# Second mixture's up products: four arms of columns instead of seven widths, and no turned path for few tokens

## The chip, the cores and the metric

The kernel runs on one core of a Trainium2 chip. The metric is the device time of one execution in microseconds; the time before is the median of three runs. The profile shows one further execution with its own time. The engines are TensorE (PE; its weight loads stand apart as PEld), VectorE (DVE), ScalarE (ACT), GpSimd (POOL) and the queue of SyncE (SP), which starts the transfers.

## The reference

Attention without softmax, a dense feed-forward layer, and a mixture of eight experts follow on each other. The change lies in the mixture:

```python
logits = x @ w_gate                       # 2304 tokens, 512 features, 8 experts
expert_idx = np.argmax(logits, axis=1)
gate_w = probs[np.arange(N), expert_idx]  # probs: softmax of the logits
for i in range(N):                        # at most capacity = 576 tokens per expert
    e = expert_idx[i]
    if counts[e] < capacity:
        disp[e, counts[e]] = x[i]; pos[i] = counts[e]; counts[e] += 1; keep[i] = True
h = np.maximum(np.einsum('ecd,edf->ecf', disp, w1), 0.0)   # up: 512 -> 1024
y = np.einsum('ecf,efd->ecd', h, w2)                       # down: 1024 -> 512
out[i] = gate_w[i] * y[expert_idx[i], pos[i]]              # for kept tokens
```

How many tokens an expert gets is known only on the chip. With these inputs the router sends 52, 625, 167, 219, 614, 160, 391 and 76 tokens to experts 0 to 7, of which at most 576 are kept. The kernel starts with an expert chosen while the tokens are still routed and goes round from there; here that is expert 1, so the order is 576, 167, 219, 576, 160, 391, 76 and 52 tokens.

## The kernel before

The first part (attention, feed-forward, routing) is not touched. In the second part each expert goes through the same code, written out once for each of the eight places e = 0 to 7. Its 1024 hidden features are eight blocks f of 128.

Products are made in a float32 type that TensorE multiplies in one pass, with each operand split into a high and a low half; a product is three passes (high by high, high by low, low by high) over four chunks of the 512 features, so 12 products of a 128x128 weight block with the tokens' columns. `part` (line 810) writes these 12 for one block f and a number of columns.

`up(e, f)` makes one block of the up product in one of three double banks of PSUM, `hb`, taken in turn. Since the number of tokens n[e] is known only at run time, `widths` writes seven arms, for 256, 304, 352, 400, 448, 512 and 576 columns (the last is two parts, 256 and 320), under a tree of three levels of comparisons; a register `off` tells the evacuation where in the bank the columns begin. `up2(e, i)` holds two blocks f and is itself one arm of a branch: with at most 128 tokens, the other arm multiplies the other way round (`turned`: the tokens are the stationary operand, 256 columns of weights the moving one), copies the result to SBUF with ScalarE and turns it back with two transposes on TensorE.

`put_g` evacuates a block: ScalarE writes the high half of relu(h) (line 874), then VectorE the low half (line 875), for all 576 columns, or 128 in the turned arm. `put_last` (line 880) has ScalarE copy the 64 columns of each half of the expert's last token tile, which are packed side by side for `down`. It waits for VectorE's half. `next_pair` splits two weight tiles of a later product: ScalarE casts them to the high half (line 190), GpSimd subtracts (line 194). `up2` is called four times for each expert, with a `next_pair` after the first three.

After the up blocks come `tr_x` (transposes of the next expert's tokens, line 789), three `next_pair`, and `down` for each token tile of 128 (24 products of 512 columns, line 907, or 16 if the tile holds at most 64 tokens), then two `next_pair`. `nothing` (line 778) is a small product for arms that have nothing to do. Place e = 0 is special: its first 256 columns were made early, and `up_rest` (columns from 256 on) runs in the arm that is taken here; the other arm holds eight calls of `up`.

All queues run in the order in which the code is written (`manual_schedule`).

Of the kernel before, what the change touches and what calls it, by code (L numbers as in the profile page):

```python
# [7 lines left out]
F32 = mybir.dt.float32  # L8
F32R = mybir.dt.float32r
BF16 = mybir.dt.bfloat16  # L10
I32 = mybir.dt.int32
I64 = mybir.dt.int64
AF = mybir.ActivationFunctionType
ALU = mybir.AluOpType
# [5 lines left out]
P = 128  # L20


PASSES = ((0, 0), (0, 1), (1, 0))
# [3 lines left out]
def attn_moe_kernel(ctx: ExitStack, tc: tile.TileContext, cap, kp, vp, qt, gn, wm, wg, wgt, w1, w2, ident, tri, out):  # L27
    nc = tc.nc
    B, NPAIR, _, NCH, _ = kp.shape
# [3 lines left out]
    KD = DM // P  # L33
    NF = wm.shape[0]
    E, NF2 = w1.shape[0], w1.shape[1] * 2
# [6 lines left out]
    NARROW, BANK, HALF = 256, 512, P // 2  # L42
# [4 lines left out]
    const = ctx.enter_context(tc.tile_pool(name="const", bufs=1))  # L47
# [7 lines left out]
    id_sb = const.tile([P, P], F32, name="id_sb")  # L55
    tri_sb = const.tile([P, 2, P], BF16, name="tri_sb")
    cnt = const.tile([P, E], F32, name="cnt")
    cnt_i = const.tile([P, E], I32, name="cnt_i")
    off_i = const.tile([P, E], I32, name="off_i")
    last_i = const.tile([P, E], I32, name="last_i")  # L60

    ek_i = const.tile([P, E], I32, name="ek_i")
# [460 lines left out]

    LAG, LEAD = 2, 4
    HOT = 9
    LEVELS = (NARROW, 304, 352, 400, 448, BANK, cap)
    units = []

    with tc.manual_schedule(engines={mybir.EngineType.SP}):
# [146 lines left out]
        for s in range(len(units)):  # L676
            j, f = units[s]
# [37 lines left out]
        v = nc.vector  # L715
# [3 lines left out]
        v.tensor_scalar(cnt, cnt, 1.0, -1.0, op0=ALU.max, op1=ALU.add)  # L719
        v.tensor_copy(last_i, cnt)  # L720
        v.tensor_scalar(last_i, last_i, 7, 7, op0=ALU.logical_shift_right, op1=ALU.logical_shift_left)
        v.tensor_scalar(off_i, cnt, float(BANK - 1), float(BANK - NARROW), op0=ALU.is_gt, op1=ALU.mult)
    ph1.close()


    g2_p = ctx.enter_context(tc.tile_pool(name="g2_p", bufs=1))
    x2_p = ctx.enter_context(tc.tile_pool(name="x2_p", bufs=1))
    xr_p = ctx.enter_context(tc.tile_pool(name="xr_p", bufs=4))
    ht_p = ctx.enter_context(tc.tile_pool(name="ht_p", bufs=1))
    me_p = ctx.enter_context(tc.tile_pool(name="me_p", bufs=2))  # L730
    wpool3.append(ctx.enter_context(tc.tile_pool(name="wpool3", bufs=2)))

# [1 line left out]
    hb = [psum[0].tile([P, 2 * BANK], F32, name=f"hb{i}") for i in range(3)]  # L734
    bk = [psum[1].tile([P, 512], F32, name=f"bk{i}") for i in range(2)]
# [3 lines left out]
    x2 = x2_p.tile([P, 2, KD, cap], F32R, name="x2")  # L739
# [18 lines left out]
    with tc.manual_schedule():  # L758
# [9 lines left out]
        ET = mybir.EngineType  # L768
# [7 lines left out]
        def nothing(ps, w):  # L776

            nc.tensor.matmul(ps[:w, :E], lhsT=tri_sb[:, 0, :w], rhs=tri_sb[:, 1, :E], start=True, stop=True)
# [20 lines left out]
        def w1_at(e, i, a, c):  # L799

            return we1[e, 2 * i + c // 2][:, a, c % 2 * 2 * P:(c % 2 + 1) * 2 * P]

        def part(e, f, h, o, w, x=x2):


            order = [(c, a, m) for c in range(KD) for a, m in PASSES]
            if f == 0:
                order = [(c, a, m) for a, m in ((0, 0), (1, 0), (0, 1)) for c in range(KD)]
            for k, (c, a, m) in enumerate(order):
                nc.tensor.matmul(  # L810
                    h, lhsT=w1_at(e, f // 2, a, c)[:, f % 2 * P:(f % 2 + 1) * P], rhs=x[:, m, c, o:o + w],
                    start=k == 0, stop=k == 3 * KD - 1,
                )

        def widths(e, levels, arm):

            mid = len(levels) // 2
            if not mid:
                return arm(levels[0])
            with tc.If(n[e] > levels[mid - 1]) as c:  # L820
                widths(e, levels[mid:], arm)
            with c.Else():
                widths(e, levels[:mid], arm)

        def up(e, f):

            h = hb[(e * NF2 + f) % 3]

            def arm(w):
                if w > BANK:  # L830
                    part(e, f, h[:, BANK - NARROW:BANK], 0, NARROW)
                    part(e, f, h[:, BANK:BANK + w - NARROW], NARROW, w - NARROW)
                else:
                    part(e, f, h[:, :w], 0, w)

            widths(e, LEVELS, arm)
            put_g(f, h[:, bass.ds(off[e], cap)], slice(0, cap))

        turned_sb = [ht_p.tile([P, 2 * P], F32, name=f"turned{i}") for i in range(2)]

        def turned(e, i):

            s = (bk[i % 2] if i else hb[e * NF2 % 3][:, BANK:])[:, :2 * P]
            order = [(c, a, m) for c in range(KD) for a, m in PASSES]
            for k, (c, a, m) in enumerate(order):
                nc.tensor.matmul(
                    s, lhsT=x2[:, a, c, :P], rhs=w1_at(e, i, m, c), start=k == 0, stop=k == len(order) - 1,
                )
            return s

        def up2(e, i):

            with tc.If(nall[e] > P) as many:  # L853
                up(e, 2 * i)
                up(e, 2 * i + 1)
            with many.Else():
                if i == 0:
                    nc.scalar.copy(turned_sb[0], turned(e, 0))
                if i + 1 < NF2 // 2:
                    s = turned(e, i + 1)  # L860
                hs = [hb[(e * NF2 + 2 * i + k) % 3][:, :P] for k in range(2)]
                for k, h in enumerate(hs):
                    nc.tensor.transpose(h, turned_sb[i % 2][:, k * P:(k + 1) * P], id_sb)
                if i + 1 < NF2 // 2:
                    nc.scalar.copy(turned_sb[(i + 1) % 2], s)
                for k, h in enumerate(hs):
                    put_g(2 * i + k, h, slice(0, P))
            for f in range(2 * i, 2 * i + 2):
                put_last(f, bass.ds(last[e], HALF))

        def put_g(f, src, cols):

            g = g2[f][:, :, cols]
            nc.scalar.activation(out=g[:, 0], in_=src, func=AF.Relu)  # L874
            nc.vector.scalar_tensor_tensor(  # L875
                out=g[:, 1], in0=src, scalar=0.0, in1=f32(g[:, 0]), op0=ALU.max, op1=ALU.subtract
            )

        def put_last(f, cols):
            nc.scalar.copy(gl[f], f32(g2[f][:, :, cols]))  # L880
# [71 lines left out]
        for f in range(3):  # L952
# [5 lines left out]
            skip_runtime_bounds_check_because="an expert has no more than all tokens",  # L958
        )
        _, n = nc.values_load_multi_w_load_instructions(  # L960
            cnt_i[0:1, :], engines=[PE], min_val=0, max_val=cap,
            skip_runtime_bounds_check_because="the counts are clamped to the capacity on the chip",
        )
        _, nall = nc.values_load_multi_w_load_instructions(
            cnt_i[0:1, :], engines=[PE, ET.Activation, ET.DVE, ET.Pool], min_val=0, max_val=cap,
            skip_runtime_bounds_check_because="the counts are clamped to the capacity on the chip",
        )

        _, off = nc.values_load_multi_w_load_instructions(
            off_i[0:1, :], engines=[ET.Activation, ET.DVE], min_val=0, max_val=BANK - NARROW,  # L970
            skip_runtime_bounds_check_because="the offsets are one of two numbers",
        )

        _, last = nc.values_load_multi_w_load_instructions(
            last_i[0:1, :], engines=[ET.Activation], min_val=0, max_val=(cap - 1) // P * P,
            skip_runtime_bounds_check_because="the counts are clamped to the capacity on the chip",
# [11 lines left out]
        for e in range(E):  # L988
            if e + 1 < E:
                for t in range(4):  # L990
                    load_x(e + 1, t)
            if e == 0:
                with tc.If(early > NARROW - 1) as done:
                    for f in range(NF2):
                        up_rest(f)
                with done.Else():
                    tr_x(0, 0)
                    tr_x(0, 1)
                    for f in range(NF2):
                        up(0, f)  # L1000
                        put_last(f, bass.ds(last[0], HALF))
            else:
                for i in range(NF2 // 2):
                    up2(e, i)
                    if i < NF2 // 2 - 1:
                        next_pair((AP, AP))
            if e + 1 < E:
                tr_x(e + 1, 0)
                tr_x(e + 1, 1)
                for t in range(4, NST):  # L1010
                    load_x(e + 1, t)
            if e:
                next_pair((AP, AP))
            next_pair((AP, AP))
            next_pair((AP, AP))
            down(e, 0)
            if e + 1 < E:
                rest_x(e + 1, range(2, NST))
            with tc.If(nall[e] > P) as some:  # L1019
                down(e, 1)  # L1020
            with some.Else():
                nothing(hb[((e + 1) * NF2 + 2) % 3], P)
            next_pair((AP, AP))
            next_pair((AP, AP))
            down_rest(e, 2)
# [50 lines left out]
```

## Time and profile before

| | before |
|---|---|
| median of 3 runs | 810.14 us (810.14 to 811.97) |
| profiled execution | 804.85 us |
| its span, first to last instruction | 803.1 us |
| mean granted TensorE clock | 0.968 of full |
| TensorE busy | 729.3 us, 91% |
| weight loads busy | 648.0 us, 81% |
| VectorE, ScalarE, GpSimd busy | 371.1, 310.5, 291.5 us |
| DMA | 102.82 MB, 128 GB/s on average |

A stage is read by its start and end in the span, the engine's busy time in it, and what ended the idle time between. "issue" means that the profile shows nothing that the engine waited for. A name in an arrow, as in [1.80 <-DVE g L875], is what the profile infers as the last thing waited for, after so many microseconds of idleness. Some matmul records can be missing, so a count of 98 may stand for a few more.

### The profile page before, as it was taken

Reading aid. Unit: us, or ns where it says so; the run is one execution under the profiler, and the core shown is the slowest. Engines: PE = TensorE matmul, PEld = TensorE weight load, DVE = VectorE, ACT = ScalarE, POOL = GpSimd, SP = SyncE. Lnnn points to the kernel's source line nnn. Section 1 sums busy time; section 2 is a strip of 40 time slices with the busy share of each in tenths; the row PEclk is TensorE's granted clock in tenths of the full one; section 3 lists DMA queues with packets and bytes.
Section 4 is the critical chain, followed back from the end, with each engine's and each line's share of the span. In section 5 each row is a group of like instructions: output and inputs, shape, how many; then the busy total and the mean of one; then the engine's idle time right before and its main releaser. Section 6 shows DMA issues by size and latency. Waiting matters only on the chain. (4 is left out here: it accounts for less than half of the span.)

```text
span 803.1 us, 12019 instructions
## 1 busy us (share of the span) xinstructions
PE 729.3 (91%) x3988; PEld 648.0 (81%) x3988; DVE 371.1 (46%) x829; ACT 310.5 (39%) x650; POOL 291.5 (36%) x288
## 2 busy tenths in 40 slices
PE   6788999999999999999999899997879997879663
PEld 6777999989999998899989788876768976777553
DVE  2999767279924943494469434202212202221101
ACT  2555454242223322322334533424635444544422
POOL 2575233030212002102104923253847373667440
PEclk9899999999999999999999999999969999999779
DMA  9937898020212012001004723353444454455400
GB/s 332 373 123 275 290 302 292 27 76 1 105 69 77 1 66 83 27 1 53 13 1 158 233 97 106 100 165 109 143 164 148 165 154 136 129 182 164 152 20 11
DMA packets 38044, 102.82 MB, mean 128 GB/s; under 512 B 4451, under 2 KB 4707, under 8 KB 37920
## 3 DMA queue, kind: packets, MB, share of 16 engines
q1 hardware_dynamic: 34912, 91.99, 35.0%
q0 software_dynamic: 3008, 9.10, 3.0%
q8 instruction: 87, 1.43, 0.8%
q14 instruction: 37, 0.30, 0.1%
HBM read 77.78 MB, written 23.91 MB: 127 GB/s over the span
## 5 line engine op out<-in xcount | busy, mean ns | idle before, releaser
L273 PE MATMUL pk<-xT,w 128*128 128x384 f32 x1152 | 223.1, 341 | 7.5 <-POOL w L183 4.6
L292 PE MATMUL pk<-w,g 128*128 128x512 f32 x864 | 218.3, 394 | 2.5 <-ACT g L284 2.5
L273 PEld LDWEIGHTS pk<-xT,w 128*128 128x128 f32 x1152 | 201.6, 188 | 17.3 <-POOL w L183 5.9
L194 POOL TENSOR_TENSOR w<-st,w 128x512 fp32r<-128x512 f32 x128 | 161.2, 1294 | 120.2 <-ACT w L190 120.2
L292 PEld LDWEIGHTS pk<-w,g 128*128 128x128 f32 x864 | 160.2, 188 | 31.7 <-ACT g L284 3.1
L810 PE MATMUL hb<-x,w 128*128 128x256 f32 (+2 forms) x672 | 105.5, 316 | 24.5 <-issue 11.3
L810 PEld LDWEIGHTS hb<-x,w 128*128 128x128 f32 x672 | 99.4, 203 | 29.9 <-issue 14.4
L875 DVE SCALAR_TENSOR_TENSOR g<-hb,g 128x576 fp32r<-128x576 f32 (+3 forms) x72 | 41.4, 586 | 147.6 <-ACT g L874 147.6
L281 ACT ACTIVATE rr<-pk 128x384 f32<-128x384 f32 x96 | 47.1, 491 | 154.2 <-PE pk L273 154.0
L283 DVE TENSOR_TENSOR pk<-pk,rr 128x384 f32<-128x384 f32 x96 | 54.0, 563 | 75.0 <-ACT rr L281 74.2
L102 POOL DMA_INDIRECT disp<-y,sli x18 | 19.0, 1058 | 173.5 <-DVE sli L409 52.9
L354 DVE SCALAR_TENSOR_TENSOR junk<-y,wgb 128x512 f32<-128x512 f32 x120 | 77.9, 684 | 0.6 <-ACT y L312 0.6
L190 ACT CAST w<-st 128x512 fp32r<-128x512 f32 x128 | 71.5, 620 | 11.6 <-DMA st<-in_w 11.2
L284 ACT CAST g<-pk 128x384 fp32r<-128x384 f32 x96 | 46.0, 479 | 72.2 <-DVE pk L283 71.8
L285 DVE TENSOR_TENSOR g<-pk,g 128x384 fp32r<-128x384 f32 x96 | 53.3, 556 | 36.3 <-ACT g L284 36.1
L183 POOL TENSOR_TENSOR w<-cf,w 128x512 fp32r<-128x512 f32 x32 | 46.8, 1481 | 61.4 <-ACT w L182 56.8
L907 PE MATMUL hb<-w,g 128*128 128x512 f32 x264 | 65.8, 407 | 3.2 <-DVEq L946 2.9
L907 PEld LDWEIGHTS hb<-w,g 128*128 128x128 f32 x264 | 50.2, 194 | 15.3 <-DVEq L946 3.2
L874 ACT ACTIVATE g<-hb 128x576 fp32r (+3 forms) x72 | 36.1, 515 | 66.3 <-PE hb L810 63.4
L102 POOL DMA_INDIRECT out<-o,meta x22 | 21.3, 968 | 56.5 <-DVEq L1019 22.6
L923 DVE SCALAR_TENSOR_TENSOR o<-bk,meta,o 64x512 f32<-64x512 f32 x3 | 2.3, 751 | 70.5 <-ACT o L922 50.6
L239 POOL TENSOR_SCALAR ms<-ss 128x8 f32<-128x8 f32 x18 | 4.6, 253 | 76.2 <-DVE ss L237 75.9
(134 smaller groups left out, 651.6 us busy)
## 6 DMA issues: line engine op xcount, KB each, us to landing
st<-in_w SPq DMA_DIRECT2D x64, 512.0 KB, 3.9
st<-in_wm SPq DMA_DIRECT2D x32, 512.0 KB, 6.9
disp<-zrow SPq DMA_DIRECT2D x9, 1028.0 KB, 11.2
xr<-disp SPq DMA_DIRECT2D x32, 257.0 KB, 4.8
k<-in_kp SPq DMA_DIRECT2D x16, 320.0 KB, 4.4
v<-in_vp SPq DMA_DIRECT2D x16, 320.0 KB, 4.1
q<-in_qt SPq DMA_DIRECT2D x18, 256.0 KB, 3.2
out<-zrow SPq DMA_DIRECT2D x9, 512.0 KB, 8.3
```

Source lines behind the costliest of these rows:

```text
L183: nc.gpsimd.tensor_tensor(w[:, 1, :], o, f32(w[:, 0, :]), op=ALU.subtract)
L190: nc.scalar.copy(w[:, 0, :], s[:, i, :])
L194: e.tensor_tensor(w[:, 1, :], s[:, i, :], f32(w[:, 0, :]), op=ALU.subtract)
L273: nc.tensor.matmul(h, lhsT=wi[f][:, a, c * P:(c + 1) * P], rhs=xT[j][:, m, c, :], start=n == 0, stop=n == 3 * KD - 1,)
L281: nc.scalar.activation(out=r, in_=h, func=AF.Relu)
L283: nc.vector.tensor_tensor(h, h, r, op=ALU.mult)
L284: nc.scalar.copy(g[:, 0, :], h)
L285: nc.vector.tensor_tensor(g[:, 1, :], h, f32(g[:, 0, :]), op=ALU.subtract)
L292: nc.tensor.matmul(ysets[j == 1][i], lhsT=g[:, a, i * P:(i + 1) * P], rhs=wo[f][:, m, :], start=f == 0 and n == 0, stop=f == NF - 1 and n ...
L354: nc.vector.scalar_tensor_tensor(out=junk, in0=yt[j * TB + i][:, :DM], scalar=1.0, in1=wgb[e // 2][:, e % 2, :], op0=ALU.mult, op1=ALU.mul ...
L810: nc.tensor.matmul(h, lhsT=w1_at(e, f // 2, a, c)[:, f % 2 * P:(f % 2 + 1) * P], rhs=x[:, m, c, o:o + w], start=k == 0, stop=k == 3 * KD - 1,)
L907: nc.tensor.matmul(ps[:k, :], lhsT=lhs(f, a), rhs=we2[e, f][:, b, :], start=n == 0, stop=n == len(passes) * NF2 - 1,)
```

## The change

The seven widths become four arms in a tree on TensorE alone: at most 128 tokens, 128 columns; else 256 columns and then, if there are more tokens, 160 further columns (up to 416) or 320 (up to 576). The turned arm, its two SBUF tiles, its transposes and copies go, as does the branch around a pair of blocks that all four compute engines took. The offset register goes, since the columns always begin at the same place. The evacuation always covers 576 columns. `put_last` of a block now stands right behind its evacuation.

```diff
-    LEVELS = (NARROW, 304, 352, 400, 448, BANK, cap)
+    MIDDLE = 416
...
-        def widths(e, levels, arm):
-
-            mid = len(levels) // 2
-            if not mid:
-                return arm(levels[0])
-            with tc.If(n[e] > levels[mid - 1]) as c:
-                widths(e, levels[mid:], arm)
-            with c.Else():
-                widths(e, levels[:mid], arm)
-
         def up(e, f):
 
-            h = hb[(e * NF2 + f) % 3]
-
-            def arm(w):
-                if w > BANK:
-                    part(e, f, h[:, BANK - NARROW:BANK], 0, NARROW)
-                    part(e, f, h[:, BANK:BANK + w - NARROW], NARROW, w - NARROW)
-                else:
-                    part(e, f, h[:, :w], 0, w)
-
-            widths(e, LEVELS, arm)
-            put_g(f, h[:, bass.ds(off[e], cap)], slice(0, cap))
...
-        def up2(e, i):
-
-            with tc.If(nall[e] > P) as many:
-                up(e, 2 * i)
-                up(e, 2 * i + 1)
-            with many.Else():
...
-            for f in range(2 * i, 2 * i + 2):
-                put_last(f, bass.ds(last[e], HALF))
+            h = hb[(e * NF2 + f) % 3][:, BANK - NARROW:]
+            with tc.If(n[e] <= P) as few:
+                part(e, f, h[:, :P], 0, P)
+            with few.Else():
+                part(e, f, h[:, :NARROW], 0, NARROW)
+                with tc.If(n[e] <= NARROW) as less:
+                    nothing(h[:, NARROW:], P)
+                with less.Else():
+                    with tc.If(n[e] <= MIDDLE) as some:
+                        part(e, f, h[:, NARROW:MIDDLE], NARROW, MIDDLE - NARROW)
+                    with some.Else():
+                        part(e, f, h[:, NARROW:cap], NARROW, cap - NARROW)
+            put_g(f, h[:, :cap], slice(0, cap))
...
                 for i in range(NF2 // 2):
-                    up2(e, i)
+                    for f in range(2 * i, 2 * i + 2):
+                        up(e, f)
+                        put_last(f, bass.ds(last[e], HALF))
                     if i < NF2 // 2 - 1:
                         next_pair((AP, AP))
```

On TensorE, one block f of an expert in the order of the program before (`hb` is the PSUM bank, `x` the tokens, `w` the weights; x12 counts the products; each stands for a weight load and a matmul):

```order
L820 COMPARE_AND_BRANCH x3
L810 MATMUL hb_4469<-x_4489,w 128x256 x12
L810 MATMUL hb_4469<-x_4489,w 128x320 x12
L820 UNCONDITIONAL_BRANCH
L810 MATMUL hb_4469<-x_4489,w 128x512 x12
L820 UNCONDITIONAL_BRANCH
...
L810 MATMUL hb_4469<-x_4489,w 128x352 x12
L820 UNCONDITIONAL_BRANCH
L810 MATMUL hb_4469<-x_4489,w 128x304 x12
L820 UNCONDITIONAL_BRANCH
L810 MATMUL hb_4469<-x_4489,w 128x256 x12
```

The same block after the change, line numbers being those of the changed kernel:

```order
L815 COMPARE_AND_BRANCH
L807 MATMUL hb_4463<-x_4484,w 128x128 x12
L815 UNCONDITIONAL_BRANCH
L807 MATMUL hb_4463<-x_4484,w 128x256 x12
L819 COMPARE_AND_BRANCH
L775 LDWEIGHTS tri_sb
L775 MATMUL hb_4463<-tri_sb 128x8
L819 UNCONDITIONAL_BRANCH
L822 COMPARE_AND_BRANCH
L807 MATMUL hb_4463<-x_4484,w 128x160 x12
L822 UNCONDITIONAL_BRANCH
L807 MATMUL hb_4463<-x_4484,w 128x320 x12
```

Eight arms of 12 products in the program became four and a dummy product; with 256 columns the arm stood last before and now stands second.

On ScalarE, the second pair of blocks of an expert before (`g` is the evacuated block, `gl` the copy for the last tile, L865 the copy of the turned arm):

```order
L874 ACTIVATE g_2_4475<-hb_4469 128x576
L874 REGISTER_ALU
L874 ACTIVATE g_3_4476<-hb_4470 128x576
L853 UNCONDITIONAL_BRANCH
L865 COPY turned_4508<-bk_4471 128x256
L874 ACTIVATE g_2_4475<-hb_4469 128x128
L874 ACTIVATE g_3_4476<-hb_4470 128x128
L853 UNCONDITIONAL_BRANCH
L880 ISA
L880 COPY gl_4483<-g_2_4475 128x128
L880 ISA
L880 COPY gl_4484<-g_3_4476 128x128
```

And after:

```order
L831 ACTIVATE g_2_4470<-hb_4464 128x576
L815 UNCONDITIONAL_BRANCH
L837 ISA
L837 COPY gl_4478<-g_2_4470 128x128
L831 ACTIVATE g_3_4471<-hb_4465 128x576
L815 UNCONDITIONAL_BRANCH
L837 ISA
L837 COPY gl_4479<-g_3_4471 128x128
```

The copies moved from behind both evacuations of a pair to behind each of them, and the arm of 128 columns is gone from ScalarE's program.

## Rows read from the trace of the kernel before

**Rows 1.** The page: TensorE's busy time, the large instruction queue, GpSimd's weight differences.

```profile
PE 729.3 (91%) x3988; PEld 648.0 (81%) x3988; DVE 371.1 (46%) x829; ACT 310.5 (39%) x650; POOL 291.5 (36%) x288
...
q8 instruction: 87, 1.43, 0.8%
...
L194 POOL TENSOR_TENSOR w<-st,w 128x512 fp32r<-128x512 f32 x128 | 161.2, 1294 | 120.2 <-ACT w L190 120.2
```

**Rows 2.** Up stages of e1, e2, e4, e5, e6: busy PE, PEld, DVE, ACT, POOL; clock; DMA.

```profile
544.80:564.40 19.60, 14.30 (x98) 13.00 (x97) 6.05 (x8) 9.61 (x20) 8.45 (x8) 0.91 0.23 67
574.70:601.40 26.70, 18.86 (x99) 17.50 (x99) 5.97 (x8) 11.88 (x24) 15.41 (x15) 0.68 0.53 172
...
667.90:688.60 20.70, 12.82 (x97) 11.77 (x96) 6.06 (x8) 9.73 (x20) 8.69 (x9) 1.00 0.26 73
699.90:723.00 23.10, 18.83 (x99) 17.14 (x98) 6.21 (x9) 12.63 (x26) 15.09 (x17) 1.00 0.60 180
744.60:764.50 19.90, 10.46 (x64) 9.16 (x63) 4.00 (x11) 11.35 (x33) 9.78 (x10) 0.76 0.43 143
```

**Rows 3.** Timeline of PE, e1's up stage and down products: start, length, instruction, idle before.

```profile
544.78 3.99 PE L810 MATMUL hb<-x,w 128*128 128x256 f32 x32
...
553.16 1.69 PE L810 MATMUL hb<-x,w 128*128 128x256 f32 x12 [1.64 <-DVE g L875]
...
562.83 1.70 PE L810 MATMUL hb<-x,w 128*128 128x256 f32 x12 [1.11 <-issue]
...
565.16 5.79 PE L907 MATMUL hb<-w,g 128*128 128x512 f32 x24
...
570.83 3.97 PE L907 MATMUL hb<-w,gl 128*128 128x512 f32 x16
```

**Rows 4.** Timeline of PE, e0's remaining columns and e3's up stage.

```profile
501.23 14.33 PE L810 MATMUL hb<-x,w 128*128 128x320 f32 x96
516.98 1.08 PE L789 MATMUL bk<-id_sb,xr 128*128 128x128 f32 x8 [1.42 <-issue]
...
614.98 25.82 PE L810 MATMUL hb<-x,w 128*128 128x256 f32 x192
```

**Rows 5.** DMA queues, windows 544.8:565.2 and 615:641.4: packets, MB, share.

```profile
q8 instruction: 6, 0.10, 2.2%
...
q8 instruction: 7, 0.11, 1.7%
```

**Rows 6.** Timeline of ScalarE and VectorE in e1's up stage: one chain.

```profile
547.85 0.65 ACT L874 ACTIVATE g<-hb 128x576 fp32r x1 [0.74 <-PE hb L810]
...
548.54 0.76 DVE L875 SCALAR_TENSOR_TENSOR g<-hb,g 128x576 fp32r<-128x576 f32 x1 [0.63 <-ACT g L874]
...
549.33 0.30 ACT L880 CAST gl<-g 128x128 fp32r x1 [0.64 <-DVE g L875]
549.53 1.14 ACT L190 CAST w<-st 128x512 fp32r<-128x512 f32 x2
```

**Rows 7.** Timeline of ScalarE from e1's last output to e2's first evacuation.

```profile
574.89 0.68 ACT L922 ACTIVATE o<-hb,meta 64x512 f32<-64x512 f32 x1 [3.17 <-PE hb L778]
...
577.96 1.19 ACT L874 ACTIVATE g<-hb 128x576 fp32r x2 [0.33 <-PE hb L810]
```

**Rows 8.** Plain float32 products on PE: two timeline rows, and line 209's group.

```profile
7.68 1.35 PE L209 MATMUL pk<-v,k 128*128 128x128 f32 x10 [0.30 <-DMA v<-in_vp]
...
483.23 1.07 PE L332 MATMUL pk<-wg_raw,yT 128*128 128x8 f32 x8 [0.46 <-ACT yT L329]
...
L209 PE MATMUL pk<-v,k 128*128 128x128 f32 x160 | 23.5, 302 | 1.4 <-DMA v<-in_vp 1.4
```

**Rows 9.** Timeline: e6's first up product, and the last output copy of e7.

```profile
745.43 1.66 PE L846 MATMUL hb<-w,x 128*128 128x256 f32 x12 [0.62 <-issue]
...
794.95 0.68 ACT L922 ACTIVATE o<-hb,meta 64x512 f32<-64x512 f32 x1 [3.00 <-PE hb L778]
```

More of the change, by code (lines that the diff above doesn't have):

```diff
@@ L58, in attn_moe_kernel @@
     cnt_i = const.tile([P, E], I32, name="cnt_i")
-    off_i = const.tile([P, E], I32, name="off_i")
     last_i = const.tile([P, E], I32, name="last_i")
@@ L721, in attn_moe_kernel @@
         v.tensor_scalar(last_i, last_i, 7, 7, op0=ALU.logical_shift_right, op1=ALU.logical_shift_left)
-        v.tensor_scalar(off_i, cnt, float(BANK - 1), float(BANK - NARROW), op0=ALU.is_gt, op1=ALU.mult)
     ph1.close()
@@ L728, in attn_moe_kernel @@
     xr_p = ctx.enter_context(tc.tile_pool(name="xr_p", bufs=4))
-    ht_p = ctx.enter_context(tc.tile_pool(name="ht_p", bufs=1))
     me_p = ctx.enter_context(tc.tile_pool(name="me_p", bufs=2))
@@ L839, in attn_moe_kernel @@
[L839 to L849, printed above, removed]
-        def up2(e, i):
-            with tc.If(nall[e] > P) as many:
-                up(e, 2 * i)
-                up(e, 2 * i + 1)
-            with many.Else():
[L857 to L867, printed above, removed]
-            for f in range(2 * i, 2 * i + 2):
-                put_last(f, bass.ds(last[e], HALF))
@@ L967, in attn_moe_kernel @@
         )
[L969 to L972, printed above, removed]
         _, last = nc.values_load_multi_w_load_instructions(
```

## The prediction, made before the changed kernel had run

> The experts are called by their place in the program, e0 to e7. Worked out from the inputs, they hold 576 (the capacity), 167, 219, 576, 160, 391, 76 and 52 tokens; a row's tile forms show which arm each takes.
>
> **What bounds the kernel now.** I read the busy shares first: TensorE (PE) is busy 729.3 of 803.1 us [rows 1], so the question is where it stands still. [...] The timeline of e1 [rows 3] shows the form of it: the first 32 products run without a gap, but later twelve products take 1.70 us and are followed by gaps of 1 to 2 us, labelled with an evacuation on VectorE or with nothing. e3, with more than twice the columns, runs its 192 products in 25.82 us without any [rows 4], though it goes through the same banks and the same evacuations of 576 columns. So evacuation is not what e1 waits for.
>
> What e1 and e3 share is the instruction stream. In e1's 20.4 us TensorE's and the others' large instruction queue brings 6 packets of together 0.10 MB, in e3's 26.4 us 7 [rows 5]. That is about one piece of 16 KB in 3.4 us, or 3.8, whichever arm is taken. In the whole run it brings 87 packets, 1.43 MB [rows 1]. By the order of instructions TensorE's program has some 23,000 of them (10,831 products of a weight load and a matmul each, and 1,400 others), the other engines have some 3,800 together; so nearly all of it is TensorE's, read from end to end, 62 bytes each and 264 to a piece. One block f of before is about 210 instructions, 8 arms of 24 and the branches: 0.8 pieces, 0.8 x 3.4 = 2.7 us. e1's 19.6 us are 2.45 per f, e4's 20.7 are 2.6. I read the gaps as TensorE jumping over six or seven arms into code that has not yet come.
>
> [...]
>
> **The change, part by part.**
>
> *Price of a product.* e0's 96 products of 320 columns take 14.33 us, 0.149 each; e3's 192, half of 320 and half of 256, take 25.82 us, 0.1345 on average, so 0.120 for 256 columns [rows 4]. For 128 and 160 columns of this type there is no row. From below: a plain float32 pass of 8 columns (x8) takes (1.07 - 0.25)/7 = 0.117 and one of 128 columns (x10) (1.35 - 0.27)/9 = 0.120 [rows 8], 0.25 and 0.27 being the part of the last one that nothing covers. A product of 8, 128 or 256 columns thus costs the same, which looks like the load of its weights. From above: the code has 80 plain products of keys and values, and the trace 160 of them [rows 8], so a plain product of 128 columns costs two passes, 0.240, and one of 160 in proportion 0.300. The weights here are loaded as in the 256 column rows, so I take the lower end, 0.120, and keep 0.240 and 0.300 for the range.
>
> *Instruction stream.* Four arms and a dummy product instead of eight arms: about 106 instructions per f, 0.40 pieces, 1.4 us at 3.4 us a piece. Twelve products of 128 or 256 columns take 1.44. The stream stops being the limit.
>
> *Evacuation.* Before, both blocks of a pair were evacuated and then both copies for the last tile were made; now copy follows evacuation for each f. On ScalarE this is a chain [rows 6]: evacuation at 547.85, VectorE's half at 548.54, copy at 549.33, next at 549.53, so 1.68 us per f, with 1.14 us for the weights' casts after each of the first three pairs. Nothing of this hides behind 1.44 us of products: it is what is late next. Three banks allow f7 to start when VectorE has finished f4. With R the first evacuation, 1.70 us after the first product, f4's evacuation is at R + 2 x (2 x 1.68 + 1.14) = R + 9.0, finished at R + 10.45; f7 ends 1.70 later. **The up stage of an expert with few columns becomes 1.7 + 10.45 + 1.7 = 13.9 us.**
>
> *The sum*, on the profiled execution:
> - e1: 19.6 [rows 2] to 13.9, -5.7.
> - e2: 26.7 [rows 2] to 13.9, -12.8, of which the clock is a part: the products come closer together, and I assume the upper level.
> - between e1 and e2 ScalarE needs 577.96 - 574.89 = 3.07 us after the last down product before it evacuates again [rows 7], and e2's first block is now ready after 1.7: +1.6 with the step before it. Larger blocks (e3, e5) cover this.
> - e4: 20.7 to 13.9, -6.8.
> - e3: same arms, 256 and 320, 0.
> - e5: 24 products of 0.120 are 2.88 per f, 23.0 us against 23.1, 0.
> - e6 and e7: from e6's first product to the last output copy before, 794.95 - 745.43 = 49.5 us [rows 9]. After: R at 1.7, eight f and three pairs of casts 16.9, then two transposed copies and six casts at 0.57 and an output of 0.7 make 5.3, so e7's first evacuation is at 23.9; eight f of 1.68 bring the last copy to 37.3, the last two products 0.4: 37.7, -11.8. TensorE itself needs 13.9 + 0.8 + 5.7 for e6 (the last two as in e1 [rows 2, 3]) and is not later. In this, wider evacuations (576 instead of 128 columns) are already counted, and the 16 transposes with their copies are gone.
> - e0's unused branch, which is jumped over at 516.98 with 1.42 us idle [rows 4], is shorter; the jump stays, 0. Eight register loads on two engines and the base of the offset go, beside other work, 0.
>
> Together -35.5: 804.85 - 35.5 = 769.3 for the profiled execution. That one is 5.3 us below the median of the runs shown, 810.14, so the median comes to 774.6. **I predict 775 us.** 0.3% is 2.4 us, about what a measurement of this kernel can tell from no change.
>
> **Rivals.**
> - *The narrow products are dear.* At 0.240 and 0.300: e5 takes 8 x 12 x (0.120 + 0.300) = 40.3, +17.2. e6's f is 2.88, so 23.0 + 0.8 + 5.7 = 29.5, and e7 23.0 + 2.1 behind it: 54.6 against 49.5, +5.1. With e1, e2, e4 at -23.7 the sum is -1.4: 809, no change; any price below this end is faster by its part. For it speaks that no row shows a product of this type under 256 columns; against it the equal prices from 8 to 256.
> - *Another engine takes the place.* GpSimd makes two differences of 1.29 us [rows 1] for each of eight pairs per expert, 20.6 us, besides the output scatters; e1 now would go round in 13.9, 565.16 - 564.40 = 0.8 for the transposes [rows 2, 3] and 5.7 and 3.9 for two down products [rows 3], 24.3 in all. If weights come late by some 4 us in e1, e2, e4 and e6, or e2 stays at its clock of 0.68 (twelve products 1.70/0.68 = 2.5, its stage some 20.5, +6.6), about half is left: 792.
> - *The gaps are evacuation waits after all*, as their label says [rows 3]. Then e1, e2 and e4 keep their times, and e6 and e7, now of the same form, need e1's 19.6 us each, with 0.8 + 5.7 between and 2.1 for the last block's chain 47.8 against 49.5 [rows 9]: -1.7, 808. Against it stands e3.
> - *Slower: jumps.* The new tree takes three jumps per f in e3 and e5 (past the arm of 128, past the dummy, past or out of the next arm) and two in e1, e2, e4. If each costs 1.42 us, as the jump over e0's branch did [rows 4], e3 needs 4.26 per f instead of 3.23, +8.2; e5 34.1, +11.0; the small ones 8 x 2.84 + 1.7 = 24.4, so +4.8, -2.3, +3.7; e6 and e7 have one jump under their 1.68, -11.8. Sum +13.6: 824. It decides from about 1.28 us per jump. Against it: before, every f of e3 ended in a jump over five arms, and its 192 products show no gap; and the new jumps are over 25 to 80 instructions, within a piece or into the next.
>
> [...]
>
> **How the numbers follow.** Chances: the forecast 0.55 (its own range 765 to 787, from a few us less in the chain of ScalarE and from e2's clock), half of it 0.13, dear products 0.15 (0.07 faster, 0.06 same, 0.02 slower), waits that stay 0.07 (0.05 same, 0.02 slower), jumps 0.10. Faster 0.75, same 0.11, slower 0.14. From 765 to 811 lie nearly all of the first three and most of the fourth; what is left out is the jumps and the tails, about 2 in 10.
>
> **What would show it.** Right: the up stages of e1, e2 and e4 near 14 us, with idle time ended by evacuations and no unlabelled gaps; fewer packets of the large instruction queue (about 25 fewer in the whole run); twelve products of 128 columns in about 1.6 us; 24 products of e5 in 2.9; the end from e6's first product to the last output copy 38 us instead of 49.5. Wrong: e5's stage at 40 us (price of narrow products); unlabelled gaps of over 1 us in e3 (jumps); stages of 20 us with the same gaps (not the stream). The step I trust least is the price of 128 and 160 columns, since it decides over 22 us.

## The result, and the profile after

The changed kernel takes **775.88 us** (median of four runs, 775.50 to 775.97). The kernel before, run beside it, takes 811.06 us (810.14 to 815.64). The ratio is 0.9555, 95% interval 0.9517 to 0.9592. The profiled execution after is of 775.5 us, 29.35 less than the 804.85 us profiled before.

The page after, with TensorE's busy time and the large instruction queue:

```profile
PE 732.8 (95%) x4188; PEld 655.8 (85%) x4188; DVE 379.6 (49%) x828; ACT 314.9 (41%) x642; POOL 292.4 (38%) x288
...
q8 instruction: 61, 1.00, 0.6%
```

TensorE is busy for 3.5 us more and stands still for 33 us less than before [rows 1]; the queue brings 61 packets instead of 87.

The up stages of e1, e2, e4, e5 and e6 after (columns as in [rows 2]: busy PE, PEld, DVE, ACT, POOL; clock; DMA):

```profile
545.60:559.10 13.50, 12.58 (x106) 12.09 (x104) 5.27 (x7) 7.67 (x16) 5.96 (x5) 1.00 0.19 55
571.50:586.50 15.00, 13.02 (x107) 12.39 (x106) 5.28 (x7) 9.73 (x20) 13.46 (x12) 1.00 0.76 240
655.10:668.60 13.50, 12.58 (x106) 12.10 (x104) 5.26 (x7) 7.67 (x16) 5.97 (x5) 1.00 0.18 53
682.00:704.20 22.20, 22.20 (x194) 22.20 (x194) 6.06 (x8) 12.41 (x25) 15.68 (x18) 1.00 0.58 195
725.60:741.90 16.30, 14.58 (x104) 13.72 (x103) 6.06 (x8) 9.67 (x21) 7.86 (x7) 0.80 0.49 164
```

e1, e2 and e4 went from 19.6, 26.7 and 20.7 us to 13.5, 15.0 and 13.5, and e2's clock from 0.68 to 1.00. The timeline of PE in e1 (to 561.99), e3, e5 and e6 shows what is left; [rows 3, 4] are the same places before:

```profile
545.56 1.60 PE L807 MATMUL hb<-x,w 128*128 128x256 f32 x12
...
554.88 1.69 PE L807 MATMUL hb<-x,w 128*128 128x256 f32 x12
...
557.51 1.71 PE L807 MATMUL hb<-x,w 128*128 128x256 f32 x12 [0.92 <-DVE g L832]
...
559.10 1.07 PE L786 MATMUL bk<-id_sb,xr 128*128 128x128 f32 x8
561.99 5.77 PE L864 MATMUL hb<-w,g 128*128 128x512 f32 x24 [1.82 <-DVE g L832]
...
602.18 25.82 PE L807 MATMUL hb<-x,w 128*128 128x256 f32 x192
...
681.96 22.44 PE L807 MATMUL hb<-x,w 128*128 128x256 f32 x192
...
725.57 7.17 PE L807 MATMUL hb<-x,w 128*128 128x128 f32 x60
733.02 3.90 PE L807 MATMUL hb<-x,w 128*128 128x128 f32 x24 [0.28 <-DVE g L832]
737.41 2.83 PE L807 MATMUL hb<-x,w 128*128 128x128 f32 x12 [0.48 <-DVE g L832]
...
741.88 7.47 PE L864 MATMUL hb<-w,g 128*128 128x512 f32 x24 [0.77 <-DVE g L832]
```

No unlabelled gap is left in e1; the two that remain end with VectorE's half of an evacuation, the second ahead of the first down product. e3 is what it was, 25.82 us, although it now takes three jumps per block. e5's 24 products take 22.44/8 = 2.81 us, and 60 products of 128 columns 7.17, 0.12 each. At the end of e6 the products of 128 columns and the down products run slower: that is the clock, 0.80 in this stage and 0.75 from 741.9 to 749.2 us.

ScalarE in e1 after (timeline), the chain that [rows 6] show before, and the last output copy:

```profile
547.23 0.65 ACT L831 ACTIVATE g<-hb 128x576 fp32r<-128x576 f32 x1 [0.79 <-PE hb L775]
...
551.63 0.64 ACT L831 ACTIVATE g<-hb 128x576 fp32r<-128x576 f32 x1
553.10 0.30 ACT L837 CAST gl<-g 128x128 fp32r x1 [0.82 <-DVE g L832]
553.30 0.65 ACT L831 ACTIVATE g<-hb 128x576 fp32r<-128x576 f32 x1
554.77 0.30 ACT L837 CAST gl<-g 128x128 fp32r x1 [0.82 <-DVE g L832]
554.98 1.14 ACT L189 CAST w<-st 128x512 fp32r<-128x512 f32 x2
556.02 0.64 ACT L831 ACTIVATE g<-hb 128x576 fp32r<-128x576 f32 x1
...
765.35 0.68 ACT L879 ACTIVATE o<-hb,meta 64x512 f32<-64x512 f32 x1 [0.83 <-PE hb L775]
```

A pair of blocks takes ScalarE 556.02 - 551.63 = 4.39 us, of which it waits twice 0.82 us for VectorE with the next evacuation queued behind the copy. From e6's first product to the last output copy there are 765.35 - 725.57 = 39.8 us, 49.5 before [rows 9].

### The profile page after: what moved, and what is told of

Its sections match the earlier page's. It is cut to its first block, busy times and chain, and to the rows that moved or that the text cites. A ratio compares the mean times of both kernels' runs of the same rounds, so it can differ in the third digit from the quotient of the medians.

```text
span 773.7 us, 12155 instructions
## 1 busy us (share of the span) xinstructions
PE 732.8 (95%) x4188; PEld 655.8 (85%) x4188; DVE 379.6 (49%) x828; ACT 314.9 (41%) x642; POOL 292.4 (38%) x288
## 5 line engine op out<-in xcount | busy, mean ns | idle before, releaser
L807 PE MATMUL hb<-x,w 128*128 128x256 f32 (+3 forms) x960 | 125.9, 290 | 5.3 <-DVE g L832 5.1
L807 PEld LDWEIGHTS hb<-x,w 128*128 128x128 f32 x960 | 122.1, 192 | 6.8 <-DVE g L832 5.5
L832 DVE SCALAR_TENSOR_TENSOR g<-hb,g 128x576 fp32r<-128x576 f32 (+2 forms) x72 | 49.8, 691 | 114.5 <-ACT g L831 114.5
L831 ACT ACTIVATE g<-hb 128x576 fp32r<-128x576 f32 (+2 forms) x72 | 42.8, 595 | 28.7 <-PE hb L807 25.3
L837 ACT CAST gl<-g 128x128 fp32r x64 | 19.1, 298 | 50.7 <-DVE g L832 50.7
```

Of the source, the lines that this page charges most:

```text
L807: nc.tensor.matmul(h, lhsT=w1_at(e, f // 2, a, c)[:, f % 2 * P:(f % 2 + 1) * P], rhs=x[:, m, c, o:o + w], start=k == 0, stop=k == 3 * KD - 1,)
L832: nc.vector.scalar_tensor_tensor(out=g[:, 1], in0=src, scalar=0.0, in1=f32(g[:, 0]), op0=ALU.max, op1=ALU.subtract)
```

## The experiments

e0 to e7 alone are places in the program, as in the prediction; an experiment always has a name behind its number. All were timed in four groups, each beside the kernel before on its own chip (e1_ to e4_: 807.46 us before, e5_ to e8_: 814.58, e9_: 811.41, e10_ and e11_: 810.45), and ratios are to that. Every kernel computes the whole. The table holds, for each, the length of TensorE's program (by the order of instructions, a product being two), the up stages of e1, e2 and e4 (first product to the next transposes), and the stretch from e6's first product to the last output copy, from the profiled executions.

| kernel | program of PE | e1 | e2 | e4 | e6 to the end | median us | ratio (95%) |
|---|---|---|---|---|---|---|---|
| before | 23,079 | 19.6 | 26.7 | 20.7 | 49.5 | 811.06 | |
| after | 15,875 | 13.5 | 15.0 | 13.5 | 39.8 | 775.88 | 0.9555 (0.9517 to 0.9592) |
| e1_pad4 | 22,147 | 18.3 | 22.7 | 20.3 | 55.5 | 811.58 | 1.0048 (1.0017 to 1.0078) |
| e2_pad2 | 19,075 | 15.2 | 15.7 | 14.7 | 52.0 | 794.43 | 0.9845 (0.9801 to 0.9890) |
| e3_three_widths | 16,423 | 12.2 | 13.1 | 12.2 | 37.0 | 759.90 | 0.9436 (0.9395 to 0.9476) |
| e4_copy_on_vector | 15,875 | 12.4 | 21.5 | 12.5 | 33.9 | 769.94 | 0.9556 (0.9505 to 0.9608) |
| e5_copies_paired | 15,875 | 12.5 | 13.0 | 12.5 | 35.5 | 762.47 | 0.9352 (0.9303 to 0.9402) |
| e6_no_turned_seven_widths | 22,211 | 16.6 | 26.8 | 19.7 | 55.3 | 807.59 | 0.9908 (0.9872 to 0.9944) |
| e7_three_widths_no_turned | 15,555 | 12.2 | 13.4 | 12.2 | 36.9 | 762.47 | 0.9367 (0.9315 to 0.9418) |
| e8_three_widths_416 | 16,423 | 12.2 | 13.1 | 12.2 | 38.3 | 761.53 | 0.9348 (0.9296 to 0.9401) |
| e9_four_single_arms | 17,219 | 12.2 | 18.3 | 12.2 | 49.9 | 777.97 | 0.9601 (0.9540 to 0.9662) |
| e10_e9_no_128_arm | 15,555 | 12.2 | 13.0 | 12.2 | 36.9 | 761.12 | 0.9397 (0.9353 to 0.9442) |
| e11_e9_dead_128_arm | 17,219 | 12.2 | 16.7 | 12.2 | 37.8 | 764.24 | 0.9443 (0.9409 to 0.9477) |

**Is it the stream of instructions?** Two experiments give the changed kernel its old length back with code that is never executed. e1_pad4:

```diff
                     with some.Else():
-                        part(e, f, h[:, NARROW:cap], NARROW, cap - NARROW)
+                        with tc.If(n[e] > 0) as always:
+                            part(e, f, h[:, NARROW:cap], NARROW, cap - NARROW)
+                        with always.Else():
+                            for _ in range(4):
+                                part(e, f, h[:, NARROW:cap], NARROW, cap - NARROW)
```

> The changed kernel with four more arms of 12 products in each up block that no number of tokens takes (a fifth way out of the tree, for an expert without tokens); nothing more is computed. A block is about 204 instructions again, as in the kernel before (about 210). If the instruction stream set the pace, a block costs 0.8 pieces of 3.4 us, some 2.6 us: the up stages of e1 and e4 go from 13.5 us back to 19 to 21, e2 from 15.0 to 20 or more, e6 and e7 lose some 8 us together, and the run comes to about 800 us (range 792 to 812) with about 86 packets on the large instruction queue. If the gaps were waits for the evacuation or came from the branch around a pair that all four engines took, nothing changes: 776 us, stages of 13.5.

e2_pad2 is the same with `range(2)`.

> The same with two arms that are never taken: about 156 instructions per block, 0.6 pieces, 2.0 us at 3.4 us a piece against 1.57 of products and dummy. Instruction stream: stages of e1, e2, e4 of 15 to 17.5 us, the run at 781 to 788 us, between the changed kernel and the one with four arms. A cost per jump instead of per piece: the same jumps as with four arms, so the same time as that one. Evacuation or common branch: 776 us.

Nothing that is executed differs in e1, e2 and e4, whose tokens never come to the new comparison. With four dead arms the gain is gone; with two, about two thirds of it (0.9845 against 0.9555). The two kernels have the same jumps, so a price per jump does not explain the difference between them. PE in e1 and e3 of e1_pad4 (timeline):

```profile
553.73 1.71 PE L807 MATMUL hb<-x,w 128*128 128x256 f32 x12 [0.57 <-issue]
...
556.77 1.71 PE L807 MATMUL hb<-x,w 128*128 128x256 f32 x12 [1.30 <-DVE g L836]
...
560.24 1.70 PE L807 MATMUL hb<-x,w 128*128 128x256 f32 x12 [1.74 <-issue]
...
611.84 25.82 PE L807 MATMUL hb<-x,w 128*128 128x256 f32 x192
```

The gaps of the kernel before are back, with the same mixed labels, and e3, which jumps over the dead arms too, still has none. The same reading in one line: the group of the 256 column products, whose last part is the idle time before them and what ended it, in after, pad4 and pad2:

```profile
L807 PE MATMUL hb<-x,w 128*128 128x256 f32 x480 | 64.5, 287 | 3.8 <-DVE g L832 3.8
```

```profile
L807 PE MATMUL hb<-x,w 128*128 128x256 f32 x480 | 67.9, 294 | 20.6 <-DVE g L836 9.5 <-issue 8.0 <-POOL w L193 1.1
```

```profile
L807 PE MATMUL hb<-x,w 128*128 128x256 f32 x480 | 65.2, 288 | 5.3 <-issue 4.3 <-DVE g L836 1.0
```

pad4's block is some 106 + 98 = 204 instructions, and e4's 20.3 us are 2.54 per block: 2.54/204 x 264 = 3.3 us for a piece of 264, beside the 3.4 that the prediction took from [rows 5]. This is an estimate; e1's 18.3 us give 3.0 in the same way, and e2's 22.7 give 3.7. The large instruction queue follows the length of the program, whether the code runs or not: 61 packets after, and in e2_pad2, e1_pad4 and e3_three_widths (the next experiment), by their pages:

```profile
q8 instruction: 72, 1.18, 0.6%
q8 instruction: 82, 1.34, 0.7%
q8 instruction: 63, 1.03, 0.6%
```

Both padded kernels also lose at the end, 15.7 and 12.2 us where some 8 were expected for e1_pad4: 60 products of 128 columns take 13.05 us in e6 of e1_pad4 (from 747 to 767 us the page's digit for the clock is 5, in tenths of full), against 7.17 after at a clock of 1.00. e2_pad2 came out above its range of 781 to 788 us by this end and by a start of e1 that is 4.5 us later (550.08 against 545.56); its up stages were in or just under theirs.

e3_three_widths asks the reverse: the kernel before with fewer widths and nothing else.

```diff
-    LEVELS = (NARROW, 304, 352, 400, 448, BANK, cap)
+    LEVELS = (NARROW, 448, cap)
```

> The kernel before with three widths (256, 448 and 576 columns) instead of seven, everything else as before: turned arm, the branch around a pair on all engines, offset register, copies for the last tile behind both evacuations of a pair. About 106 instructions per block. Instruction stream: the up stages of e1, e2, e4 fall from 19.6, 26.7 and 20.7 to 12.5 to 14.5 us, e5 (now 448 columns, 12 products of about 0.21 us, 2.5 per block) to 20 to 22, and the run to 765 to 782 us. If the turned arm or the branch on all engines made the gaps, it stays at 805 to 813 us.

It is 16 us under the changed kernel, on another chip; the intervals of the two ratios don't meet. Its turned arm, offset register and paired copies are those of before, so the number of arms alone gives all that the change gave, and more. It is also under its expected range of 765 to 782 us, since e1, e4 and e5 (19.8 us) came out just under theirs and the end, for which nothing was forecast, fell from 49.5 to 37.0 us.

**What is left: the place of the copy.** e4_copy_on_vector takes the copy for the last tile from ScalarE's chain.

```diff
-            nc.scalar.copy(gl[f], f32(g2[f][:, :, cols]))
+            nc.vector.tensor_copy(gl[f], f32(g2[f][:, :, cols]))
...
-            last_i[0:1, :], engines=[ET.Activation], min_val=0, max_val=(cap - 1) // P * P,
+            last_i[0:1, :], engines=[ET.DVE], min_val=0, max_val=(cap - 1) // P * P,
```

> The changed kernel with the copies for the last tile on VectorE instead of ScalarE, so that ScalarE's evacuation of a block no longer waits for VectorE's half of the block before. If the chain of 1.68 us per block on ScalarE is what is late in the changed kernel, the gaps of 0.9 to 1.0 us before the last blocks go (e1 and e4 12.6 us, e2 12.8), the wait of 1.8 us before the first down product falls below 0.8, and e7's eight blocks come at TensorE's pace of 1.4 instead of 1.68: 8 to 11 us less, 765 to 768 us. If TensorE or the weights bound these stages by now, less than 3 us.

e1 and e4 go to 12.4 and 12.5 us and in both the wait ahead of the first down product goes, but e2 takes 21.5 us, and the median of 769.94 us is above the 765 to 768 expected. VectorE and GpSimd there (timelines, then PE):

```profile
573.71 0.76 DVE L832 SCALAR_TENSOR_TENSOR g<-hb,g 128x576 fp32r<-128x576 f32 x1 [2.16 <-ACT g L831]
574.50 8.19 DVE L837 CAST gl<-g 128x128 fp32r x1
...
583.40 0.23 DVE L837 CAST gl<-g 128x128 fp32r x1
```

```profile
572.76 9.85 POOL L193 TENSOR_TENSOR w<-st,w 128x512 fp32r<-128x512 f32 x8
```

```profile
583.42 2.93 PE L807 MATMUL hb<-x,w 128*128 128x256 f32 x12 [7.18 <-DVE g L832]
```

One copy of 0.23 us lasts 8.19 and ends at 582.69, where GpSimd's eight subtractions end (582.61). TensorE waits 7.18 us, and the next twelve products take 2.93 us instead of 1.7.

e5_copies_paired leaves the copies on ScalarE, but puts both of a pair behind both evacuations, where they stood before the change.

```diff
                     for f in range(2 * i, 2 * i + 2):
                         up(e, f)
+                    for f in range(2 * i, 2 * i + 2):
                         put_last(f, bass.ds(last[e], HALF))
```

> The changed kernel with the two copies for the last tile of a pair again behind both evacuations of the pair; nothing else is moved. Theory (with the stream out of the way, ScalarE's order of copies and evacuations sets what is left): the up stages of e1 and e4 go from 13.5 us to about 12.5, the wait of 1.8 us before the first down product to about 0.9, e6's first product to the last output copy from 39.8 to about 37.5, the median from 775.9 to 767 to 771. Rival (the stream of instructions still sets the 13.5 us): e1 and e4 keep 13.5 us and the waits move elsewhere, 774 to 777.

ScalarE (timeline) and the 256 column products (group) of this kernel:

```profile
551.02 1.19 ACT L831 ACTIVATE g<-hb 128x576 fp32r<-128x576 f32 x2
552.49 0.30 ACT L837 CAST gl<-g 128x128 fp32r x1 [0.28 <-DVE g L832]
553.15 0.30 ACT L837 CAST gl<-g 128x128 fp32r x1 [0.36 <-DVE g L832]
553.36 1.14 ACT L189 CAST w<-st 128x512 fp32r<-128x512 f32 x2
554.40 1.19 ACT L831 ACTIVATE g<-hb 128x576 fp32r<-128x576 f32 x2
```

```profile
L807 PE MATMUL hb<-x,w 128*128 128x256 f32 x480 | 64.0, 287 | 0.2
```

A pair takes 554.40 - 551.02 = 3.38 us instead of 4.39, because the second evacuation runs while VectorE works on the first. TensorE's idle time ahead of these products goes from 3.8 to 0.2 us, and the profiled execution from 775.5 to 763.6. This is more than was expected (762.47 us for 767 to 771): e1 and e4 give 2.1 us each (half in the stage, half in the wait ahead of the first down product), e2 3.0 in the same way, and the end 4.3, of which 1.7 is e6's first down group (5.77 us for 7.47, where the clock was 0.75).

**The turned arm and the widths apart.** e6_no_turned_seven_widths and e7_three_widths_no_turned are the kernel before, and e3_three_widths, each with `up2` as two plain calls and `turned` taken out:

```diff
         def up2(e, i):
-            with tc.If(nall[e] > P) as many:
-                up(e, 2 * i)
-                up(e, 2 * i + 1)
-            with many.Else():
...
+            up(e, 2 * i)
+            up(e, 2 * i + 1)
             for f in range(2 * i, 2 * i + 2):
                 put_last(f, bass.ds(last[e], HALF))
```

> The kernel before without its turned arm: few tokens run through the arm of 256 columns, the seven widths stay. Theory (jumped-over code sets the pace): e6 and e7 become like e1, some 19 us for each up stage, 47 to 50 us from e6's first product to the last output copy as before; the code is a tenth shorter for each block, worth at most 0.2 us per block in e1, e2 and e4, so 800 to 809, beside a kernel before of 803 to 812 in the same call. Rival (the turning itself, with its transposes and copies, made e6 and e7 slow): e6 and e7 come to about 40 us as after the change, 9 to 10 us under the kernel before of the same call.

> The kernel before with three widths (256, 448, 576) and without its turned arm: few tokens run through the arm of 256 columns. Theory: with the stream out of the way the turned arm is worth little either way, since few tokens need 12 products of 0.12 us per block one way or the other and ScalarE's chain sets the pace: e6's first product to the last output copy stays within 2 us of the 37.0 us with the turned arm; the median is 757 to 763, beside 759.9 with it. Rival (the turned arm is a gain of its own for few tokens, since its evacuations are of 128 columns and not 576): e6 and e7 take 40 us or more, 763 to 768.

Without the turned arm but with seven widths, the end is not shorter: 55.3 us (mean clock 0.92 from 700 to 775 us), where 47 to 50 were expected. Its median is 0.9% below that of the kernel before on its chip. Where that gain lies is not shown: e1 and e4 are shorter (16.6 and 19.7 us), but its profiled execution is of 807.91 us, longer than the 804.85 of the kernel before, which was profiled on another occasion. With three widths the turned arm makes no difference: 36.9 against 37.0 us at the end. So few tokens were slow before for the same reason as the others, not for the turning.

e8_three_widths_416 has `LEVELS = (NARROW, 416, cap)` in e3_three_widths.

> The kernel before with three widths as before but 416 in place of 448 columns in the middle. Theory: only e5 (391 tokens) goes through this arm; its 96 products of 448 columns took 19.83 us, in proportion 416 take 18.4, so 1.4 us less: 758 to 759 beside 759.9. Rival (e5's blocks are held by the stream or the evacuation at 2.4 us each): e5 keeps 19.8 us, no change.

e5's stage takes 18.48 us instead of 19.83, as expected, but its end takes 38.3 us instead of 37.0, and the spans are 758.6 and 758.0 us, on two chips; 1.4 us can't be told there.

**An arm of 128 columns.** e9_four_single_arms has four widths, each an arm of its own (576 still in two parts of 256 and 320), without the turned arm; the arm of 128 columns is 12 products, with its branches 26 instructions more per block: `LEVELS = (P, NARROW, 416, cap)`.

> The kernel before without its turned arm and with the four widths 128, 256, 416 and 576, each of them one arm (so 24 more products in the program for each block than with three widths), both copies of a pair behind both evacuations as before. Theory: as the kernel with paired copies, but e5's middle arm is 12 products of 416 columns (18.5 us for the stage) instead of 24 of 256 and 160 (22.4 us), 3.9 us less than the 762.5 us there: 757 to 761. Rival (the added arm makes the code of a block, 5 times 12 products and the branches, long enough to be waited for again): e1 and e4 go from 12.5 to 13.5 us and over with unlabelled gaps, 763 to 768.

The theory failed by 17 us, and not where the rival had put it: e1 and e4 stay at 12.2 us. Places e6 and e7 on PE (timeline), and three stretches of e6 (windows; the clock is third from the end):

```profile
720.01 4.21 PE L810 MATMUL hb<-x,w 128*128 128x128 f32 x36
725.42 12.05 PE L810 MATMUL hb<-x,w 128*128 128x128 f32 x60 [1.20 <-issue]
...
748.28 16.55 PE L810 MATMUL hb<-x,w 128*128 128x128 f32 x84 [1.54 <-ACT g L849]
```

```profile
725.40:730.00 4.60, 4.58 (x26) 4.58 (x27) 1.51 (x2) 2.97 (x8) 2.77 (x3) 0.63 0.29 86
730.00:734.00 4.00, 4.00 (x21) 4.00 (x21) 1.51 (x2) 1.61 (x5) 2.15 (x2) 0.50 0.33 92
734.00:738.00 4.00, 4.00 (x21) 4.00 (x21) 0.76 (x1) 2.24 (x5) 2.75 (x4) 0.50 0.23 89
```

After a gap of 1.2 us the clock falls, from 1.00 before it (720.0 to 725.4 us) to 0.63 behind it and then to 0.50, where it stays for the rest of the stage (730 to 738 us), though TensorE is busy throughout. Two kernels take this apart. e10_e9_no_128_arm is `LEVELS = (NARROW, 416, cap)`; e11_e9_dead_128_arm keeps the program, but never takes the arm:

```diff
-            with tc.If(n[e] > levels[mid - 1]) as c:
+            with tc.If(n[e] > (levels[mid - 1] if levels[mid - 1] > P else 0)) as c:
```

> The kernel with the four single arms (777.97 us) without its arm of 128 columns: few tokens run through the arm of 256. In that kernel e6 and e7 ran half of their products at the lower clock after gaps of 1.2 and 1.5 us, and e2 had unlabelled gaps of 1.8 us. Theory (the arm of 128 columns is the cause, by its code or by its products): e2 is without unlabelled gaps again, e6's first product to the last output copy goes back from 50 to about 37 us, 759 to 763 us. Rival (something else in that kernel, the arm of 416 columns or the chip of that call): 770 us and over.

> The kernel with the four single arms (777.97 us), with its arm of 128 columns still in the program, instruction for instruction, but never taken: the comparison ahead of it asks for more than 0 tokens, so few tokens run through the arm of 256 columns. Theory A (the length of the code: 26 instructions more per block make TensorE wait at e2, e6 and e7, and the clock falls behind the gaps, whatever the width): e2 keeps its gaps of 1 to 2 us, e6's first product to the last output copy stays near 50 us, 774 to 780 us. Theory B (the products of 128 columns themselves hold the clock down after a gap): e2 keeps its gaps (about 4 to 5 us), but e6 and e7 run at the full clock, about 37 to 40 us, 763 to 769 us. Theory C (the jump to the arm that stands last in the code is what waits, and the arm of 256 columns now stands earlier): e2 as before, e6 and e7 without gaps of over 1 us, 763 to 767 us.

Without the arm, 761.12 us: nothing else in that kernel was at fault. With the arm dead, 764.24; PE in places e2 and e6 of it (timeline):

```profile
574.11 0.28 PE L810 MATMUL hb<-x,w 128*128 128x256 f32 x1 [2.07 <-issue]
574.88 7.50 PE L810 MATMUL hb<-x,w 128*128 128x256 f32 x48 [0.49 <-issue]
...
715.64 4.55 PE L810 MATMUL hb<-x,w 128*128 128x256 f32 x36
720.62 7.81 PE L810 MATMUL hb<-x,w 128*128 128x256 f32 x60 [0.43 <-DVE g L850]
```

e2 keeps an unlabelled gap of 2.07 us and takes 16.7 us instead of 13.0, so its cause is the dead arm, 1,664 instructions more in the whole program. The medians differ by 764.24 - 761.12 = 3.1 us, but their executions overlap (763.6 to 767.7 and 759.8 to 765.5 us). The other 13.7 us come from taking the arm: with it the clock is 0.68 in e6 (720 to 738 us) and 0.64 in e7 (745.1 to 764.6), with 256 columns it is 1.00 in both (715.6 to 730 and 735.9 to 749.5). But the gap of 1.2 us ahead of the fall is gone as well, perhaps because the arm that few tokens now take stands earlier in the code. Whether the width or the gap decides was not separated, but the width alone does not: e5_copies_paired runs 60 products of 128 columns in 6.93 us at a clock of 1.00 (717.8 to 729.8 us), with gaps of 0.2 and 0.5 us, and in place e6 of e6_no_turned_seven_widths twelve products of 256 columns took 2.93 us instead of 1.7 behind gaps of 2.56 and 1.02:

```profile
748.10 2.08 PE L810 MATMUL hb<-x,w 128*128 128x256 f32 x12 [2.56 <-ACT w L190]
751.20 2.93 PE L810 MATMUL hb<-x,w 128*128 128x256 f32 x12 [1.02 <-issue]
```

## Why the prediction was right, point by point

- **What bounds the kernel: right.** The gaps come with the length of the program around the code that runs. Dead code alone brings them back (e1_pad4), fewer arms alone take them away (e3_three_widths), and the pace of 3.4 us per piece held as an estimate (3.3 from e4 of e1_pad4, 3.0 to 3.7 over e1, e2 and e4). That TensorE waits there for code that has not yet come is the author's reading of this and of the packets; no view shows the wait itself.
- **Price of a product: right.** 0.12 us at 128 columns, and e5's 24 products 2.81 us against 2.88. The rival of dear narrow products is dead, as are the jumps (e3 has none of the gaps that 1.42 us each would give) and the evacuation waits.
- **The chain on ScalarE: right, but followed one step too short.** The up stage came out at 13.5 us against 13.9, and the last block starts when f4's evacuation is done. The step that failed is the 0.8 us from there to the first down product: that product uses f6's bank, and so waits for f6's evacuation, 1.82 us. With the transposes that is 561.99 - 559.10 = 2.9 us, 2.1 more than taken, in each of e1, e2 and e4. The 1.6 us that the prediction put between e1 and e2 lie in e2's stage: its first evacuation starts at 574.64, 3.1 us after the first product instead of 1.7, and the stage takes 15.0 us.
- **e6 and e7: right in direction, -9.7 instead of -11.8.** The terms left out the clock: 0.80 in e6, and a down group of 7.47 us that took 5.79 in e1 before [rows 3]. TensorE needed 749.28 - 725.57 = 23.7 us for e6 where the terms had 13.9 + 0.8 + 5.7 = 20.4; the wait of 0.77 us for f6's evacuation is in it too. So it was TensorE, and not ScalarE alone, that set when e7 began.
- **e5: 0 forecast, -1.9 measured** from its first product to e6's (45.54 before, 725.57 - 681.96 = 43.61 after): 0.8 in the up stage, the rest behind it.
- **The sum and the median.** By the starts of the stages: e1 0.8 later, e1 -4.0, e2 -9.6, e3 0, e4 -5.1, e5 -1.9, e6 and e7 -9.7, together -29.4 with 0.2 more behind the last output copy, where the prediction had -35.5. It came out at 775 all the same because of its last step: it added 5.3 us between the profiled execution and the median, as before, and after the change that difference is 0.4. Two errors of 6.1 and 4.9 us cancelled, which is luck: the profiled execution was forecast at 769.3 us and took 775.5. On medians the gain is 811.06 - 775.88 = 35.2 us.
- **Packets: right**, 26 fewer (about 25 forecast).
- **The rival of another engine** did not come: no up stage of e1, e2 or e4 waits for GpSimd's weights, and e2 ran at a clock of 1.00. The prediction's sum had assumed this for e2, because its products come closer together; no run shows that as the cause, only 0.68 before and 1.00 after. What stayed is the chain on ScalarE that the prediction itself had in its sum, and part of it comes from the change, through the place of the copy: with the copies paired the kernel is at 0.9352 (0.9303 to 0.9402) of before, below the interval of the change itself.

Five versions (e3_three_widths, e5_copies_paired, e7_three_widths_no_turned, e8_three_widths_416 and e10_e9_no_128_arm) end within 759.9 to 762.5 us and beat both kernels; which of them is best can't be told from these runs.

## What to carry to other kernels

Code for cases that don't occur is not free where the case that does is short (here four dead arms took the ratio from 0.9555 to 1.0048): count the instructions per block against the pace of the instruction queue (here an estimated 3.0 to 3.7 us for 264), and look for unlabelled gaps that a longer case in the same code does not have. When a wait is removed, follow the chain that is late next to its very end, over every bank that the next stage reuses, not just to the end of the stage. An engine that copies what another engine has just made holds up all that is queued behind the copy (here ScalarE waited 0.82 us at each copy); put independent work between.

## What the runs showed of the hardware

- In e4_copy_on_vector a VectorE copy from SBUF to SBUF, which takes 0.23 us elsewhere in the stage, lasted 8.19 us, to 582.69, while GpSimd made eight subtractions in a row that ended at 582.61. Later in the same stage a copy beside two subtractions (589.28, 2.53 us in all) lasted 1.14 us, from 589.52 to 590.66, about the end of the first of them. What decides between the two was not tested, nor what held the copies. VectorE's evacuation, which reads PSUM, took 0.76 us beside the eight subtractions (573.71).
- With four single arms, places e1 and e4 ran without unlabelled gaps and e2, with the same code, had two of 1.8 us, so the block's code alone does not decide whether the gaps come. What does was not tested: e2 follows other work, and its transfers were heavier (DMA share 0.73 from 569 to 588 us, against 0.21 from 546 to 558 in e1 and 0.23 from 655 to 668 in e4).
- With four single arms, products of 128 columns that followed each other without a gap went on at a clock of 0.50 (730 to 738 us) after a gap of 1.2 us; 60 of them took 12.05 us instead of the 7.17 of the changed kernel at 1.00.
